# Attention blocks whose first score pairs are computed early: how many pairs go through VectorE, when, and where two output splits stand

## The chip, the cores and the metric

The kernel runs on one core of one Trainium2 chip. The metric is the device time of one execution in microseconds. Before the change it is 1400.34 us, the median of three runs (1400.21 to 1401.76). Everything said of single instructions comes from one profiled execution, which took 1400.11 us; its span, from the first to the last instruction of the program, is 1398.2 us.

## What is computed

The input x is 2048 tokens by 512 features in float32. It is layer-normalised; the result feeds a 32-head attention with head size 16 and a SwiGLU feed-forward of width 1792, and the output is a gated residual:

```python
x = A_x
xn = _layernorm(x, axis=-1)
s = _A_ref(xn, A_wqkv, A_wo)          # softmax attention, 32 heads, then @ wo
g = _silu(_B_ref(xn, B_w_gate, B_w_up, B_w_down))   # (silu(xn@gate) * (xn@up)) @ down
return x + s * g
```

## The kernel before, in words

After a prologue (normalisation and the q, k, v projections) the kernel goes through 32 attention **units** u. A unit is one group of four heads (8 groups) for one block of 512 queries (4 blocks). The 16 key tiles of a unit are cut into three **blocks** of 4 to 6 key tiles; that makes 96 blocks, numbered `now` = 0 to 95 (line 1038). In the last four units the blocks have 6, 6, 4 or 4, 6, 6 key tiles.

A block (`run`, line 963) handles 2n **score pairs**, two for each of its n key tiles; a pair is the scores of two heads for 128 keys and 512 queries. A pair takes one of two ways:

- **direct** (D): TensorE writes both heads' scores into one of two score slots, each two PSUM banks (`scored`, line 950), and ScalarE reads the slot and writes the exponentials to SBUF (line 954). The next pair but one needs the same slot again.
- **copied** (A, then B): TensorE writes one head's scores into a single spare bank, `acc[1]`; VectorE copies them to SBUF (line 1010); TensorE writes the other head's scores into the same bank, and VectorE copies those (line 1016). The exponential is taken in SBUF after all direct pairs of the block (line 1024).

In between TensorE does **fill** steps (F): a pair of matmuls on the upper and lower half of the array that belong to the feed-forward (line 187) or, in the last eight blocks, to the output projection (`project_out`, line 380). At the block's end come the value products of the block's key tiles (`values`, line 405, matmuls at line 409).

The order of D, A, B and F in a block is not written out by hand. `events` (line 511) gives each of them a mark on a scale of fill steps, sorts the marks, and puts fill steps in between. `f` is the number of fill steps of the block, `ahead` the number of pairs already computed. The fill steps per block are 11 and 10 in blocks 86 and 87, 18 in block 88, 24 in blocks 89, 90, 91, 94, 95 and 12 in 92 and 93.

Five blocks have score pairs put ahead (`begins`, line 493): 86, 87, 88, 92 and 93. Their first two direct pairs (`begin`, line 959) are computed between the value products of the block before: all its key tiles but the last, then the two pairs, then the last key tile (lines 1031 to 1034). Blocks 86, 87, 92 and 93 have four key tiles, block 88 has six.

VectorE's other work is kept in a list, `chores`, with a cost for each in fill steps. A chore is issued when the list of copies due (`copying`) leaves room for it (line 1020), or after the last copy of the block. Among the chores are:

- the finish of a unit (`normalise`, line 412): a transpose out of PSUM (line 420), a reciprocal (425), a product (429), and for every second group another transpose (445) with a split of the result (459, 456).
- the **output splits** (`split_out`, line 325): a [128, 512] part of the attention output is split into a rounded part (a cast) and a remainder (a subtraction, line 329) for block b of queries and quarter c. `out_splits` (line 354) says in which block each is issued, at the first A of that block.

`project_out(b)` multiplies these parts with the output weights. Block 88 holds 18 steps for the last block of queries, blocks 89 and 90 those of b = 0, blocks 91 to 93 those of b = 1, blocks 94 and 95 those of b = 2. Each product is made in two passes with the halves of the array swapped between the two banks; between the passes VectorE makes two copies of one element each (`turned_over`, line 384), and TensorE's second pass waits for them. After the second pass VectorE reads the banks (line 363) and GpSimd adds the residual (line 364). The parts are loaded from memory by `load_out` (line 308).

Of the kernel before, what the change touches and what calls it, by code (L numbers as in the profile page):

```python
# [51 lines left out]
def tile_block(ctx: ExitStack, tc: tile.TileContext, x, wqkv, wo, w_gate, w_up, w_down, out):  # L52
# [272 lines left out]
    def split_out(b, c):  # L325
        dst, src = lhs[b, c], parts_o[b, c]

        def rest():
            dve.tensor_sub(dst[1], src, dst[0].bitcast(F32))
            ready.add((b, c))  # L330

        chores.append((2, partial(dve.tensor_copy, dst[0], src)))
        chores.append((3, rest))
# [18 lines left out]
            load_gate()  # L352

    def out_splits():
        for b, c in {early: ((0, 0), (0, 1), (0, 2)), early + 2: ((1, 0), (1, 1)), early + 3: ((1, 2),),
                     early + 4: ((2, 0),), early + 5: ((2, 1),), early + 6: ((2, 2),)}.get(now, ()):
            split_out(b, c)
        if now == len(blocks) - 1:
            for j in range(EARLY):
                gate_rest(j)  # L360
# [39 lines left out]
    def gate_rest(t):  # L400
        chores.append((3, partial(dve.scalar_tensor_tensor, facc[:, t], facc[:, t], 0.5, gate[t], op0=ALU.mult, op1=ALU.mult)))
        chores.append((3, partial(dve.tensor_add, facc[:, t], facc[:, t], last[t])))
# [68 lines left out]
    now = -1  # L471
# [18 lines left out]
    early = len(sizes)  # L490
# [20 lines left out]
    def events(n, f, ahead):  # L511
        length = 2 * n - ahead + f
        need = 2 * n - max(2, (10 * length + 46) // 40)
        fit = 2 if ahead else (10 * length + 55) // 112
        copied = max(0, min(need, fit)) if now else 0
        direct = 2 * n - copied
        gap = max(4, min(5, (length - 8) / max(1, direct - 2)))
        marks = [] if ahead else [(0, "D"), (1, "D")]
        marks += [((0.5 if ahead else 7) + gap * i, "D") for i in range(direct - 2)]
        marks += [(2.2 + max(5.6, min(8, (length - 5) / (2 * copied))) * i, "AB"[i % 2]) for i in range(2 * copied)]  # L520
        marks.sort(key=lambda mark: mark[0] - 0.6 * (mark[1] == "D"))
        out = []
        at = left = 0
        for t, kind in marks:
            while left < f - (kind != "D") and at < t:
                out.append((at, "F"))
                left += 1
                at += 1
            out.append((at, kind))
            at += 1 if kind == "D" else 0.5  # L530
        return direct, out + [(at + i, "F") for i in range(f - left)]

    with ExitStack() as pro:
# [251 lines left out]
        copied = list(range(16))  # L785
# [155 lines left out]
    now = 0  # L941
# [21 lines left out]
    def run(u, first, n):  # L963
        nonlocal lower
        f = sizes.pop(0) if sizes else 0
        direct, todo = events(n, f, len(begun))
        if now == 0:
            for _ in range(4):
# [22 lines left out]
        for at, (t, e) in enumerate(todo):  # L991
            if at == final and not copying:
                tidy()
            if e == "F":
                fill(1)
            elif e == "D":
                probs[straight[done]] = scored(u, done % 2, *straight[done])
                done += 1
                if done == 2:
                    unit_end()  # L1000
            elif e == "A":
                if now > early and not turned_in:
                    turned_in.append(now)
                    out_splits()
                kt, j = copies.pop(0)
                waiting.append((kt, j))
                scores(u, spare_bank, kt, j, 0)
                lower = True
                probs[kt, j] = ppool.tile([P, 2, TB], F32, tag="pr", name="pr")
                dve.tensor_copy(probs[kt, j][:, 0], spare_bank)  # L1010
                free = copying.pop(0) + 3
            else:
                kt, j = waiting[-1]
                scores(u, spare_bank, kt, j, 1)
                lower = False
                dve.tensor_copy(probs[kt, j][:, 1], spare_bank)  # L1016
                free = copying.pop(0) + 3
# [8 lines left out]
        if not turned_in:  # L1026
            out_splits()
            tidy()
# [9 lines left out]
    for now, (u, first, n) in enumerate(blocks):  # L1038
        g, b = divmod(u, NB)
# [101 lines left out]
```

## Time and profile before

| | before |
|---|---|
| median of three runs | 1400.34 us |
| profiled execution | 1400.11 us |
| span of the profile | 1398.2 us |
| TensorE busy | 1388.8 us (99%) |
| ScalarE busy | 1087.9 us (78%) |
| VectorE busy | 760.9 us (54%) |
| GpSimd busy | 73.9 us (5%) |
| granted TensorE clock, mean | 1.000 |

Rows of a timeline give the start (us from the span's start), the duration, the engine (PE TensorE, ACT ScalarE, DVE VectorE, POOL GpSimd, SPq the queue of SyncE), the line of the kernel, the operation, what it writes and reads, and the count of merged instructions; in square brackets stands idle time of the engine ahead of it and what ended it. Matmuls overlap one another, so a step's cost is the distance of two starts and not the duration. Rows of the waits view give the waiting instruction, what released it, the sum, the count and the longest wait.

### The profile page before, as it was taken

The numbers are of one execution on the slowest core, as the hardware profiler recorded it, in microseconds if no ns is written. First come the engines' busy times: TensorE is split into PE (matmuls) and PEld (weight loads), VectorE is DVE, ScalarE is ACT, GpSimd is POOL, SyncE is SP. The second block draws the span as 40 slices with busy tenths as digits, with TensorE's granted clock in tenths as the row PEclk, the third lists the DMA queues.
The fourth block names the chain that finished last, engine by engine and source line by source line (L and its number), as shares of the span: only waits on it lengthen the run. The fifth ranks groups of instructions, "written<-read, shape, count | busy, mean of one in ns | idle before, by whom it ended". The sixth has DMA issues, their size and how long they took to land.

```text
span 1398.2 us, 27653 instructions
## 1 busy us (share of the span) xinstructions
PE 1388.8 (99%) x11193; PEld 848.9 (61%) x11193; DVE 760.9 (54%) x1299; ACT 1087.9 (78%) x1245; POOL 73.9 (5%) x92
## 2 busy tenths in 40 slices
PE   9999999999999999999999999999999999999998
PEld 7777755655665565566556556655565565564655
DVE  6674555455645653556445645554565446566454
ACT  6753678877888887787888778778877887788775
POOL 4200200000000000000000000000000000000222
PEclk9999999999999999999999999999999999999999
DMA  7778741043634511254514303356224112224323
GB/s 228 271 247 264 179 100 43 15 116 84 134 80 118 118 43 36 59 131 95 136 51 110 92 13 73 82 143 145 62 69 115 34 45 73 66 88 140 126 69 143
DMA packets 126953, 148.13 MB, mean 106 GB/s; under 512 B 12524, under 2 KB 79340, under 8 KB 126052
## 3 DMA queue, kind: packets, MB, share of 16 engines
q1 hardware_dynamic: 121620, 125.79, 34.9%
q0 software_dynamic: 4912, 20.12, 3.9%
q8 instruction: 89, 1.46, 0.4%
q14 instruction: 44, 0.36, 0.1%
q10 hardware_dynamic: 288, 0.39, 0.1%
HBM read 106.68 MB, written 39.58 MB: 105 GB/s over the span
## 4 chain that ended last, share of the span: by engine, by line
PE 87%; ACT 1%; DVE 1%; issue 0%; DVEq 0%; ACTq 0%
PE acc L409 32%; PE bankx L187 23%; PE score L948 16%; PE banky L187 9%; PE acc L948 3%; PE bankx L380 1%; ACT pr L954 1%; PE banky L380 1%; DVE pr L1010 0%; PE acc L1078 0%; PE bankx L1078 0%; DVE hh L1022 0%; PE score L1078 0%; DVE pr L1016 0%; DVE y L1085 0%
## 5 line engine op out<-in xcount | busy, mean ns | idle before, releaser
L954 ACT ACTIVATE pr<-score 128x1024 f32<-128x1024 f32 x857 | 810.2, 1032 | 226.2 <-PE score L948 224.3
L409 PE MATMUL acc<-pr,vst 128*17 128x512 f32 x4096 | 459.1, 593 | 0.0
L948 PE MATMUL score<-qst,kst 50*128 50x512 f32 x1714 | 393.5, 413 | 0.2 <-ACT pr L954 0.2
L187 PE MATMUL bankx<-fx,guh 64*128 64x512 f32 x896 | 333.3, 393 | 0.1
L187 PE MATMUL banky<-fx,guh 64*128 64x512 f32 x896 | 324.7, 393 | 0.0
L409 PEld LDWEIGHTS acc<-pr,vst 128*17 128x17 f32 x4096 | 110.0, 97 | 290.6 <-issue 271.0
L948 PEld LDWEIGHTS score<-qst,kst 50*128 50x128 f32 x1714 | 174.5, 184 | 143.9 <-issue 70.6
L1010 DVE COPY pr<-acc 128x512 f32<-128x512 f32 x167 | 115.5, 691 | 187.4 <-PE acc L948 183.6
L187 PE MATMUL bankx<-wd,hh 64*128 64x512 f32 x672 | 201.6, 392 | 0.0
L187 PE MATMUL banky<-wd,hh 64*128 64x512 f32 x672 | 198.3, 393 | 0.0
L187 PEld LDWEIGHTS bankx<-fx,guh 64*128 64x128 f32 x896 | 166.5, 186 | 18.7 <-issue 0.9
L187 PE MATMUL banky<-fx,gul 64*128 64x512 f32 x448 | 175.5, 392 | 0.0
L187 PE MATMUL bankx<-fx,gul 64*128 64x512 f32 x448 | 175.3, 391 | 0.0
L1024 ACT ACTIVATE pr<-pr 128x1024 f32<-128x1024 f32 x167 | 171.3, 1078 | 1.1 <-DVE turned_over L384 0.5
L187 PEld LDWEIGHTS banky<-fx,guh 64*128 64x128 f32 x896 | 166.4, 186 | 5.0
L1016 DVE COPY pr<-acc 128x512 f32<-128x512 f32 x167 | 115.4, 691 | 75.2 <-PE acc L948 61.4
L948 PE MATMUL acc<-qst,kst 50*128 50x512 f32 x334 | 134.4, 403 | 2.3 <-DVE pr L1010 2.2
L240 DVE SCALAR_TENSOR_TENSOR ga<-th,bankx 128x512 f32<-128x512 f32 x56 | 38.5, 687 | 178.5 <-ACT th L239 178.5
L187 PEld LDWEIGHTS bankx<-wd,hh 64*128 64x128 f32 x672 | 124.9, 186 | 13.9 <-DVE fx L1022 0.9
L187 PEld LDWEIGHTS banky<-wd,hh 64*128 64x128 f32 x672 | 124.3, 186 | 3.3
L187 PEld LDWEIGHTS bankx<-fx,gul 64*128 64x128 f32 x448 | 83.6, 187 | 10.1
L187 PEld LDWEIGHTS banky<-fx,gul 64*128 64x128 f32 x448 | 83.5, 186 | 2.7
(186 smaller groups left out, 1298.9 us busy)
## 6 DMA issues: line engine op xcount, KB each, us to landing
gur<-in_B_w_gate_dram SPq DMA_DIRECT2D x56, 256.0 KB
gur<-in_B_w_up_dram SPq DMA_DIRECT2D x56, 256.0 KB
wdr<-in_B_w_down_dram SPq DMA_DIRECT2D x56, 256.0 KB
kst<-k_d SPq DMA_DIRECT2D x192, 64.0 KB
qst<-q_d SPq DMA_DIRECT2D x192, 64.0 KB
fx<-xt_d SPq DMA_DIRECT2D x24, 512.0 KB
q_d<-parts SPq DMA_DIRECT2D x16, 512.0 KB
k_d<-parts SPq DMA_DIRECT2D x16, 512.0 KB
```

The source lines that it names most:

```text
L187: mm(banks[i], lhs[halves[i]], rhs[halves[i]], start=start, stop=stop)
L240: dve.scalar_tensor_tensor(ga, th, 1.0, bankx, op0=ALU.add, op1=ALU.mult)
L380: mm(banks[k], lhs[b, c][a][halves[h], (j + k) * P:(j + k + 1) * P], fx[halves[h], w, c], start=swap == i == 0, stop=i == 3 * n - 1, skip_ ...
L409: mm(acc[0][h * 32:h * 32 + DH + 1], v[:, kt % CT, h * (DH + 1):(h + 1) * (DH + 1)], probs[kt, h // 2][:, h % 2], start=kt == 0, stop=kt = ...
L948: mm(bank, k[r, j, kc * P:(kc + 1) * P], qst[u % 2][r, j], start=True, stop=True)
L954: act(pr, score[slot], AF.Exp, scale=0.25)
L1010: dve.tensor_copy(probs[kt, j][:, 0], spare_bank)
L1016: dve.tensor_copy(probs[kt, j][:, 1], spare_bank)
L1024: act(probs[kt, j], probs[kt, j], AF.Exp, scale=0.25)
```

## The change

Two places change. In `out_splits` the split (2, 0) moves from block 92 to block 91, (2, 1) from 93 to 92 and (2, 2) from 94 to 93. In `events`, for a block with pairs put ahead, the number of copied pairs becomes n - 3, and the first copied half gets the mark 0.3 instead of 2.2. Other blocks keep their marks.

```diff
     def out_splits():
-        for b, c in {early: ((0, 0), (0, 1), (0, 2)), early + 2: ((1, 0), (1, 1)), early + 3: ((1, 2),),
-                     early + 4: ((2, 0),), early + 5: ((2, 1),), early + 6: ((2, 2),)}.get(now, ()):
+        for b, c in {early: ((0, 0), (0, 1), (0, 2)), early + 2: ((1, 0), (1, 1)), early + 3: ((1, 2), (2, 0)),
+                     early + 4: ((2, 1),), early + 5: ((2, 2),)}.get(now, ()):
             split_out(b, c)
...
     def events(n, f, ahead):
         length = 2 * n - ahead + f
         need = 2 * n - max(2, (10 * length + 46) // 40)
-        fit = 2 if ahead else (10 * length + 55) // 112
-        copied = max(0, min(need, fit)) if now else 0
+        fit = (10 * length + 55) // 112
+        copied = n - 3 if ahead else max(0, min(need, fit)) if now else 0
         direct = 2 * n - copied
         gap = max(4, min(5, (length - 8) / max(1, direct - 2)))
         marks = [] if ahead else [(0, "D"), (1, "D")]
         marks += [((0.5 if ahead else 7) + gap * i, "D") for i in range(direct - 2)]
-        marks += [(2.2 + max(5.6, min(8, (length - 5) / (2 * copied))) * i, "AB"[i % 2]) for i in range(2 * copied)]
+        marks += [((0.3 if ahead else 2.2) + max(5.6, min(8, (length - 5) / (2 * copied))) * i, "AB"[i % 2]) for i in range(2 * copied)]
```

`early` is 88. Before the change the marks of the five blocks with pairs put ahead come out as follows (F fill, D direct pair, A and B the two halves of a copied pair):

```
86: F D F A F D F F F B D F F F D A F B F
87: F D F A F D F F F B D F F F D A B F
88: F D F A F D F F F D B F F F A D F F D F F B F D F F F D F D
92, 93: F D F A F D F F F B D F F F D A F F B F
```

## The prediction

> **What bounds the kernel now.** I read the page first (busy time, then the chain), then the waits of the stretch that the change touches, then the rows of TensorE (PE), ScalarE (ACT) and VectorE (DVE) in it.
>
> ```profile
> PE 1388.8 (99%) x11193; PEld 848.9 (61%) x11193; DVE 760.9 (54%) x1299; ACT 1087.9 (78%) x1245; POOL 73.9 (5%) x92
> ...
> PE 87%; ACT 1%; DVE 1%; issue 0%; DVEq 0%; ACTq 0%
> ```
>
> TensorE is busy 99% of the span and carries 87% of the chain that ended last. So an edit is worth what it takes out of TensorE's own queue as waiting, and nothing else. The diff reaches only the blocks whose first two score pairs are put ahead (86, 87, 88, 92, 93 of 96) and the output splits in blocks 91 to 94. All of that lies between 1261 and 1372 us. In that stretch the waits view says:
>
> ```profile
> PE acc L948 <- DVE pr L1010: 2.2, 4, 0.9
> ```
>
> TensorE waited four times for a VectorE copy out of the spare bank, once at the end of each of the four short blocks. TensorE's rows, with a block's first fill matmul, the late copied half, and the first value product:
>
> ```profile
> 1262.79 0.50 PE L187 MATMUL bankx<-wd,hh 64*128 64x512 f32 x1
> ...
> 1263.12 0.40 PE L948 MATMUL score<-qst,kst 50*128 50x512 f32 x2
> ...
> 1266.26 0.39 PE L948 MATMUL acc<-qst,kst 50*128 50x512 f32 x1
> ...
> 1267.44 0.50 PE L948 MATMUL acc<-qst,kst 50*128 50x512 f32 x1 [0.55 <-DVE pr L1010]
> ...
> 1268.10 2.77 PE L409 MATMUL acc<-pr,vst 128*17 128x512 f32 x24
> ...
> 1272.45 0.50 PE L187 MATMUL bankx<-wd,hh 64*128 64x512 f32 x1
> ...
> 1277.07 0.49 PE L948 MATMUL acc<-qst,kst 50*128 50x512 f32 x1 [0.85 <-DVE pr L1010]
> ...
> 1277.73 2.77 PE L409 MATMUL acc<-pr,vst 128*17 128x512 f32 x24
> ...
> 1282.08 0.50 PE L380 MATMUL bankx<-fx,part 64*128 64x512 f32 x1
> ...
> 1289.47 0.49 PE L948 MATMUL score<-qst,kst 50*128 50x512 f32 x2 [0.16 <-ACT pr L954]
> ```
>
> ```profile
> 1289.90 5.34 PE L409 MATMUL acc<-pr,vst 128*17 128x512 f32 x48
> ```
>
> ```profile
> 1338.56 0.50 PE L380 MATMUL bankx<-fx,wd 64*128 64x512 f32 x1
> ...
> 1340.08 0.39 PE L380 MATMUL bankx<-fx,wd 64*128 64x512 f32 x1
> ...
> 1340.54 0.39 PE L380 MATMUL bankx<-fx,wd 64*128 64x512 f32 x1
> ...
> 1343.25 0.49 PE L948 MATMUL acc<-qst,kst 50*128 50x512 f32 x1 [0.38 <-DVE pr L1010]
> ...
> 1343.91 2.77 PE L409 MATMUL acc<-pr,vst 128*17 128x512 f32 x24
> ...
> 1348.26 0.49 PE L380 MATMUL bankx<-fx,wd 64*128 64x512 f32 x1
> ...
> 1352.93 0.50 PE L948 MATMUL acc<-qst,kst 50*128 50x512 f32 x1 [0.39 <-DVE pr L1010]
> ...
> 1353.60 3.63 PE L409 MATMUL acc<-pr,vst 128*17 128x512 f32 x32
> ```
>
> From first fill to first value product a block now takes 5.31 us (86), 5.28 (87), 7.82 (88), 5.35 (92) and 5.34 (93). The next block's first fill follows 4.35 us later (1268.10 to 1272.45, 1277.73 to 1282.08, 1343.91 to 1348.26), since only value products and the two pairs ahead lie between; I keep that stretch as it is. A step (one fill pair, or one direct score pair) takes 0.23 us: 1340.08 to 1340.54 is two. The first step takes 0.33 (1262.79 to 1263.12). So step k of a block starts 0.33 + 0.23 x (k - 1) after its first fill. From the last direct pair to the value products it is 0.43 (1289.47 to 1289.90). A copied half takes half a step.
>
> **The change part by part.** Copied pairs become key tiles less three: 2 become 1 in the four blocks of four tiles, and 2 become 3 in block 88, which has six. Work on TensorE stays the same, as two halves are one step, like a direct pair. What moves is who waits for whom. VectorE and ScalarE:
>
> ```profile
> 1266.69 0.69 DVE L1010 COPY pr<-acc 128x512 f32<-128x512 f32 x1
> ```
>
> ```profile
> 1271.42 5.80 ACT L954 ACTIVATE pr<-score 128x1024 f32<-128x1024 f32 x6 [1.61 <-PE score L948]
> ```
>
> ```profile
> 1263.90 3.77 ACT L954 ACTIVATE pr<-score 128x1024 f32<-128x1024 f32 x4 [0.19 <-ACT pr L954]
> ```
>
> ```profile
> 1272.64 0.72 DVE L420 STREAM_TRANSPOSE o<-acc 128x512 f32<-128x512 f32 x1 [3.97 <-PE acc L409]
> ...
> 1273.39 0.25 DVE L425 RECIPROCAL rl<-o 128x16 f32<-128x16 f32 x1
> ```
>
> The spare bank's round is 1.18 us: half at 1266.26, copy at 1266.69, next half at 1267.44. Exps of direct pairs follow one another every 0.95 us (six in 5.80, one being 1.03), the first starting 1.03 us before the first fill (1271.42 against 1272.45). A direct pair uses a score slot that the exp two before it must have left.
>
> Block 86. The mark list of the new code, worked out by hand, is F D A F F D F B F F D F F F D F F D (F fill, D direct pair, A and B the copied halves). A stands at step 2 (0.56 us), B at step 6.5 (1.60), but the bank is free at 0.56 + 1.18 = 1.74: a wait of 0.14. The last D stands at step 16: 3.78 + 0.14 = 3.92. Its slot is free when the fifth exp ends: -1.03 + 4 x 0.95 + 1.03 = 3.80. No wait. Value products at 3.92 + 0.43 = 4.35 against 5.31: **0.96 gained**. If the third exp is late by 0.2 as at 1263.90, it is 0.75.
>
> Block 87, one F fewer. It opens with the finish of the last unit: transpose and reciprocal hold VectorE until 1273.64, 1.19 after the first fill, ahead of A's copy, which then ends at 1.92; B goes at 1.98 instead of 1.60, and TensorE, having drained, loses 0.10 more (0.33 for 0.23): 0.48. The third D is at step 9: 2.17 + 0.48 = 2.65; its exp starts after its 0.40 and about 0.1 for the hand-over (an estimate), at 3.15, and ends at 4.18. The last D (step 15, 3.55 + 0.48 = 4.03) waits for that slot until 4.20. Value products at 4.63 against 5.28: **0.65 gained**, between 0.3 and 1.0. What is late next is ScalarE, not the bank.
>
> Blocks 92 and 93 have one fill more between A and B. In 92, B is at step 7.5 (1.83), after 1.74: no wait; last D at step 17, 4.01; value products at 4.44 against 5.35: **0.91 gained**. 93 opens with a finish as 87 does: B at 1.98 for 1.83, so 0.15; 4.59 against 5.34: **0.75 gained**.
>
> Block 88 gets a third copied pair, list F D A F F D F B F F D F F A F D F F D B F F F D F A F D F B F. Three things happen. The first B waits 0.14 as in 86. The second A (step 12, 2.86 + 0.14 = 3.00) stands just ahead of the ninth fill, which ends the first pass of the output product; behind that fill TensorE needs the two tiny copies that turn the banks over (row 1328.17 below, 0.15 each), and these now queue on VectorE behind A's copy: 3.00 + 0.43 + 0.69 = 4.12, with the two about 4.35. TensorE would be at the tenth fill (step 14.5) at 3.58, so 0.8 of waiting and 0.1 for the restart. The third A (step 23) comes at 5.39 + 1.04 = 6.43, its B is due 3.5 steps (0.8) later but the bank is free only at 7.61, and from there to the value products it is 0.66 (1267.44 to 1268.10): 8.27 against 7.82: **0.45 lost**. Bounds: 0.9 lost if the two waits add to those that it has now, 0.5 gained if the turn-over gets ahead. Its twelve exps, the three out of SBUF last, end at -1.03 + 12 x 0.95 = 10.4 if fed without a gap; the last key tile's products begin at 8.27 + 5/6 of 5.34 = 12.7, so the third copied pair's exp costs nothing there unless it falls 2 us behind.
>
> The splits of the second block's and the third block's outputs (line 355): (2, 0) goes from block 92 to 91, (2, 1) from 93 to 92, (2, 2) from 94 to 93. Each is a cast and a subtraction on VectorE; no DMA is moved.
>
> ```profile
> 1357.73 0.39 PE L380 MATMUL bankx<-fx,hh 64*128 64x512 f32 x1
> ...
> 1366.56 5.34 PE L409 MATMUL acc<-pr,vst 128*17 128x512 f32 x48
> ```
>
> ```profile
> 1372.41 0.39 PE L380 MATMUL bankx<-fx,hh 64*128 64x512 f32 x1
> ```
>
> ```profile
> 1380.73 0.62 PE L409 MATMUL acc<-pr,vst 128*17 128x512 f32 x4
> ```
>
> ```profile
> 1290.56 0.42 DVE L143 CAST hh<-hh 128x512 fp32r<-128x512 f32 x1
> ```
>
> ```profile
> 1359.07 1.66 DVE L1022 CAST hh<-hh 128x512 fp32r<-128x512 f32 x1
> ```
>
> ```profile
> 1359.13 1.30 POOL L364 TENSOR_TENSOR pair<-facc,pair 128x512 f32<-128x512 f32 x1
> ```
>
> ```profile
> 1326.58 0.68 DVE L1016 COPY pr<-acc 128x512 f32<-128x512 f32 x1
> ...
> 1328.17 0.15 DVE L384 COPY turned_over<-bankx 1x1 f32<-1x1 f32 x1 [0.91 <-PE bankx L380]
> ```
>
> Block 94 needs 8.83 us to its value products, block 95, with the same marks and no such split, 8.32. In 94 the cast took 1.66 instead of 0.42, beside a GpSimd addition, and the fills that read its result queue behind it. With the split gone to 93, 94 should be like 95: **0.5 gained** (8.83 - 8.32); the lower bound is 0, if another wait stands behind it. In block 91 the added cast and subtraction start after the copy that ends at 1327.26 and end near 1328.4 (0.42 + 0.69), so the turn-over at 1328.17 comes up to 0.2 later, beside one copied half and one direct pair that cover part: **0.1 lost**, between 0 and 0.3. In 92 and 93 a split merely takes another's place.
>
> The Trainium skill, "SBUF — State Buffer", section "SBUF: two separate sides", says that VectorE and GpSimd share one port pair by an exclusive lock, held for a whole instruction. The stretched cast agrees: 1.66 us, ending 0.30 after GpSimd's addition ended at 1360.43. By that rule a moved split pays again wherever it meets such an addition; what this would cost is the second rival.
>
> The sum: 0.96 + 0.65 + 0.91 + 0.75 - 0.45 - 0.1 + 0.5 = **3.2 us**, 0.23%. The profiled execution took 1400.11 us (span 1398.2 and 1.9 around it), 0.23 below the median of 1400.34; I take the sum from the median: 1397.1.
>
> **The rivals.** First: ScalarE takes the bank's place. In a short block seven pairs instead of six now need a score slot. If exps follow at 1.22 (1.03 + 0.19, as before 1263.90) and not at 0.95, the fifth ends at 4.88, the value products start at 5.3, and the four blocks gain nothing; if half of them do so, about 1.6 us stay: 1398.7. For it speaks the 0.16 wait at 1289.47; against it the six exps in 5.80.
>
> Second: the slow cast moves along with the split. If a GpSimd addition met (2, 0) or (2, 2), that cast would again be 1.24 longer, and the 0.5 would be paid there: 3.2 - 0.5 = 2.7, 1397.6; were it to hold up a turn-over by the 0.8 worked out for block 88, 1.9, 1398.4. Against it: the additions wait for the output product's last bank reads, which in block 93 come behind the split in VectorE's queue.
>
> Third, slower: the split (2, 0) comes before its data.
>
> ```profile
> 1315.94 1.29 SPq L312 DMA_DIRECT2D hh<-o_d x3
> ```
>
> ```profile
> out_dram<-pair POOLq DMA_DIRECT2D x10, 256.0 KB, 2.9
> ```
>
> In block 91 it would read about 1327.3, 11.4 us after the load was issued (it now does so in block 92). A late landing would hold VectorE, and behind it the spare bank's copies and the turn-over, so TensorE, one for one. It takes back the gain at 14.6 us from issue and makes the kernel slower by over 0.2% at 17.4: 1403.1 or more. The nearest landing of that size is 2.9 us, so it is unlikely.
>
> Fourth: the change does not do what it says, because the waits at the block ends only pass to the next value products: 1400.
>
> **How the numbers follow.** Forecast as worked out: 0.70, of which 0.60 gains over 0.2% (2.8 us, about what a measurement of this kernel can tell from no change) and 0.10 less. First rival 0.16, second 0.06, third 0.04, fourth 0.04. That makes faster 0.60, same 0.10 + 0.16 + 0.06 + 0.04 = 0.36, slower 0.04. The terms at their ends (86: 0.6 to 1.0, 87: 0.3 to 1.0, 92: 0.7 to 0.95, 93: 0.5 to 0.95, 88: -0.9 to 0.5, 91: -0.3 to 0, 94: 0 to 0.5), not all at once, give a gain of about 1.4 to 4.3: 1396.0 to 1398.9, which takes in the likelier half of the first rival.
>
> **What would show it.** Right: the four waits of TensorE for the copy at line 1010 are gone; blocks 86, 87, 92, 93 take about 4.4, 4.6, 4.4, 4.6 us to their value products; 94 takes 8.3 with no cast over 0.5; 88 takes about 8.3 with a wait behind the turn-over. Wrong: the short blocks stay above 5 us with waits on ScalarE's exps, 88 loses over 1 us, or a cast of 1.6 shows in 91 to 93.

## The result, and the profile after

The changed kernel takes 1397.34 us (median of 14 runs, 1396.67 to 1398.52) against 1400.28 us for the kernel before, measured beside it (14 runs). The ratio is 0.9979, 95% interval 0.9971 to 0.9987: 2.9 us faster. The forecast was 1397.1, its range 1396.0 to 1398.9. The profiled execution took 1397.09 us, its span is 1395.3 us.

The page's first line and first engine of the changed kernel, and then what its waits view says of TensorE in the stretch 1262 to 1384 us (waiting instruction, releaser, sum, count, longest):

```profile
span 1395.3 us, 27643 instructions
...
PE 1387.7 (99%) x11193; PEld 849.8 (61%) x11193; DVE 755.9 (54%) x1293; ACT 1087.4 (78%) x1245; POOL 73.7 (5%) x92
```

```profile
PE bankx L380 <- DVE turned_over L384: 0.4, 1, 0.4
```

TensorE has as many instructions as before, VectorE six fewer: two copies less in each of four blocks, two more in block 88. The entry "PE acc L948 <- DVE pr L1010" with its four waits is gone, and a wait behind the turn-over is there instead. Now the ends of the short blocks in TensorE's timeline: first fill, last direct pair, first value product of blocks 86 and 87, and the first fill of 88.

```profile
1262.80 0.50 PE L187 MATMUL bankx<-wd,hh 64*128 64x512 f32 x1
...
1264.54 0.49 PE L948 MATMUL acc<-qst,kst 50*128 50x512 f32 x1
...
1264.88 0.40 PE L187 MATMUL banky<-wd,hh 64*128 64x512 f32 x1
...
1266.74 0.40 PE L187 MATMUL banky<-wd,hh 64*128 64x512 f32 x1
1266.92 0.50 PE L948 MATMUL score<-qst,kst 50*128 50x512 f32 x2
1267.35 0.62 PE L409 MATMUL acc<-pr,vst 128*17 128x512 f32 x4
...
1271.69 0.49 PE L187 MATMUL bankx<-wd,hh 64*128 64x512 f32 x1
...
1275.87 0.50 PE L948 MATMUL score<-qst,kst 50*128 50x512 f32 x2
1276.30 0.62 PE L409 MATMUL acc<-pr,vst 128*17 128x512 f32 x4
```

A direct pair now stands last, and 0.43 us behind it the value products begin. Block 88, at its turn-over and its end, on TensorE and then on VectorE:

```profile
1280.65 0.50 PE L380 MATMUL bankx<-fx,part 64*128 64x512 f32 x1
...
1283.68 0.49 PE L948 MATMUL acc<-qst,kst 50*128 50x512 f32 x1
...
1284.15 0.49 PE L948 MATMUL score<-qst,kst 50*128 50x512 f32 x2
1285.01 0.50 PE L380 MATMUL bankx<-fx,part 64*128 64x512 f32 x1 [0.37 <-DVE turned_over L384]
...
1287.05 0.45 PE L948 MATMUL acc<-qst,kst 50*128 50x512 f32 x1
...
1288.28 0.50 PE L948 MATMUL acc<-qst,kst 50*128 50x512 f32 x1
...
1288.93 0.62 PE L409 MATMUL acc<-pr,vst 128*17 128x512 f32 x4
```

```profile
1284.21 0.69 DVE L1010 COPY pr<-acc 128x512 f32<-128x512 f32 x1
1284.82 0.14 DVE L384 COPY turned_over<-bankx 1x1 f32<-1x1 f32 x1
1284.88 0.13 DVE L384 COPY turned_over<-banky 1x1 f32<-1x1 f32 x1
```

The copy of the second A (1283.68) runs until 1284.90, the two tiny copies end at 1285.01, and only then does the tenth fill start, although the direct pair before it started at 1284.15. The third A at 1287.05 and its B at 1288.28 are a bank round of 1.23 us apart. Last, block 94:

```profile
1355.30 0.39 PE L380 MATMUL bankx<-fx,hh 64*128 64x512 f32 x1
```

```profile
1363.63 0.62 PE L409 MATMUL acc<-pr,vst 128*17 128x512 f32 x4
```

From first fill to first value product, read in this way from each trace (us):

| block | 86 | 87 | 88 | 91 | 92 | 93 | 94 |
|---|---|---|---|---|---|---|---|
| before | 5.31 | 5.28 | 7.82 | 8.32 | 5.35 | 5.34 | 8.83 |
| forecast | 4.35 | 4.63 | 8.27 | 8.4 | 4.44 | 4.59 | 8.33 |
| after | 4.55 | 4.61 | 8.28 | 8.40 | 4.59 | 4.59 | 8.33 |
| splits alone | 5.32 | 5.28 | 7.80 | 8.40 | 5.33 | 5.34 | 8.34 |
| pairs alone | 4.56 | 4.61 | 8.27 | 8.32 | 4.57 | 4.59 | 8.31 |
| count alone | 4.48 | 4.31 | 8.29 | 8.40 | 4.43 | 4.47 | 8.35 |
| mark alone | 4.96 | 5.08 | 8.17 | 8.40 | 5.11 | 5.12 | 8.33 |
| short blocks only | 4.50 | 4.32 | 7.60 | 8.40 | 4.42 | 4.46 | 8.34 |
| 88 past the turn-over | 4.55 | 4.60 | 7.69 | 8.39 | 4.59 | 4.60 | 8.33 |
| copy ahead of the finish | 4.54 | 4.54 | 8.44 | 8.39 | 4.58 | 4.58 | 8.36 |
| exps of one head (86, 87) | 4.49 | 4.25 | 8.30 | 8.39 | 4.56 | 4.58 | 8.34 |
| best | 4.49 | 4.32 | 7.31 | 8.33 | 4.43 | 4.47 | 8.33 |

The stretch from these first value products to the next block's first fill is nearly the same in every trace: 4.33 to 4.36 us behind blocks 86, 87 and 92, as assumed, and 4.13 behind 93. The differences between the rows before and after add up to 0.76 + 0.67 - 0.46 - 0.08 + 0.76 + 0.75 + 0.50 = 2.90 us, which is the whole difference of the spans (1398.2 - 1395.3). So the table can stand for the time; it is the finer measure too, since in the traces here the first value products of all come between 162.8 and 164.0 us, and single times carry that difference.

### The profile page after: what moved, and what is told of

It is laid out like the page before. It is cut to its first block, busy times and chain, and to the rows that moved or that the text cites. A ratio compares the mean times of both kernels' runs of the same rounds, so it can differ in the third digit from the quotient of the medians.

```text
span 1395.3 us, 27643 instructions
## 1 busy us (share of the span) xinstructions
PE 1387.7 (99%) x11193; PEld 849.8 (61%) x11193; DVE 755.9 (54%) x1293; ACT 1087.4 (78%) x1245; POOL 73.7 (5%) x92
## 4 chain that ended last, share of the span: by engine, by line
PE 88%; ACT 0%; DVE 0%; issue 0%; DVEq 0%
PE acc L409 32%; PE bankx L187 23%; PE score L948 17%; PE banky L187 10%; PE acc L948 3%; PE bankx L380 2%; PE banky L380 1%; ACT pr L954 0%; PE acc L1078 0%; PE bankx L1078 0%; PE score L1078 0%; DVE pr L1010 0%; DVE y L1085 0%; DVE pr L1016 0%; DVE fx L1022 0%
## 5 line engine op out<-in xcount | busy, mean ns | idle before, releaser
L948 PE MATMUL score<-qst,kst 50*128 50x512 f32 x1720 | 395.4, 412 | 0.1
L948 PEld LDWEIGHTS score<-qst,kst 50*128 50x128 f32 x1720 | 176.3, 184 | 142.5 <-issue 66.3
L1010 DVE COPY pr<-acc 128x512 f32<-128x512 f32 x164 | 113.3, 691 | 188.1 <-PE acc L948 186.0
L1024 ACT ACTIVATE pr<-pr 128x1024 f32<-128x1024 f32 x164 | 168.0, 1078 | 0.0
L1016 DVE COPY pr<-acc 128x512 f32<-128x512 f32 x164 | 113.3, 691 | 74.9 <-PE acc L948 65.9
L948 PE MATMUL acc<-qst,kst 50*128 50x512 f32 x328 | 131.9, 402 | 0.1
```

Source lines behind the costliest of these rows:

```text
L948: mm(bank, k[r, j, kc * P:(kc + 1) * P], qst[u % 2][r, j], start=True, stop=True)
L1024: act(probs[kt, j], probs[kt, j], AF.Exp, scale=0.25)
```

## The experiments

**The two edits apart.** The first kernel is that before with only line 355 of the change, the second the changed one with line 355 as before.

```diff
-early + 3: ((1, 2),), early + 4: ((2, 0),), early + 5: ((2, 1),), early + 6: ((2, 2),)
+early + 3: ((1, 2), (2, 0)), early + 4: ((2, 1),), early + 5: ((2, 2),)
```

> The kernel before with only the output splits moved. Theory (each term stands by itself: block 94 loses 0.5 us because its split's cast is stretched beside a GpSimd addition, and no other block can suffer the same): block 94 takes 8.3 us from its first fill to its value products instead of 8.83, block 91 at most 0.1 more, all other blocks as before; time about 0.4 us below the kernel before, 1399.9. Rival (the stall passes to the block that takes the split): 94 takes 8.3, but 92 or 93 takes 0.3 to 0.5 more than 5.35 and 5.34, and the time is that of before.

> The changed kernel with the output splits where they were before. Theory: blocks 86, 87, 92, 93 take 4.55, 4.61, 4.58, 4.59 us to their value products and 88 takes 8.28, as in the changed kernel, and 94 is at 8.8 again; time about 2.5 us below the kernel before, 1397.8. Rival (the two edits need each other, since the shorter blocks 92 and 93 leave VectorE less room for the splits): one of 92, 93, 94 takes over 0.3 more than that, gain under 2.2.

Splits alone: 1399.78 us, ratio 0.9998 (0.9989 to 1.0007); that interval does not tell 0.4 us from nothing, but the table does: 94 at 8.34, 91 0.08 longer, the others as before. Pairs alone: 1397.37 us, ratio 0.9980 (0.9970 to 0.9989), as fast as the whole change. And here both the theory and its rival fall: block 94 takes 8.31 us although it still holds its split. GpSimd's and VectorE's rows of the kernel with the pairs alone:

```profile
1353.52 1.27 POOL L364 TENSOR_TENSOR pair<-facc,pair 128x512 f32<-128x512 f32 x1 [16.61 <-DVE facc L363]
...
1355.67 1.29 POOL L364 TENSOR_TENSOR pair<-facc,pair 128x512 f32<-128x512 f32 x1
```

```profile
1356.38 0.69 DVE L1010 COPY pr<-acc 128x512 f32<-128x512 f32 x1 [2.35 <-PE acc L948]
1356.98 0.42 DVE L1022 CAST hh<-hh 128x512 fp32r<-128x512 f32 x1
```

The cast takes 0.42 us. With two copies fewer in block 93, VectorE reads the output banks earlier (line 363 from 1352.75, 2.9 us ahead of block 94's first fill, against 1.5 before the change), GpSimd's second addition starts 0.03 us after block 94's first fill (1355.64) instead of 1.4 after it (1359.13 against 1357.73), and it ends at 1356.96, 0.03 ahead of the cast at 1356.98. So the two edits take away the same 0.5 us, and each would do it without the other.

**Is it GpSimd's addition that stretches the cast?** The kernel before, with two residual additions left out:

```diff
-        pool.tensor_add(xr[t], gt[t % NT], xr[t])
-        (pool if t < end - 1 else sp).dma_start(out[rows[t]], xr[t])
+        if t in (6, 7):
+            pool.dma_start(out[rows[t]], gt[t % NT])
+        else:
+            pool.tensor_add(xr[t], gt[t % NT], xr[t])
+            (pool if t < end - 1 else sp).dma_start(out[rows[t]], xr[t])
```

> The kernel before, with the last two residual additions of the second block of queries left out (its two tiles are stored without x), so that GpSimd adds nothing while block 94 begins; splits and pairs as before. Theory (the cast in block 94 is stretched only because a GpSimd addition runs beside it): the cast takes 0.42 us, and block 94 takes 8.3 instead of 8.83; time 0.5 below the kernel before. Rival (the cast waits for its data or for memory traffic, or the split in this block costs TensorE by itself): the cast stays above 1 us, or 94 stays above 8.6.

In the kernel before, TensorE's ninth and tenth fill of block 94, the tenth being the first that reads this split:

```profile
1360.33 0.39 PE L380 MATMUL bankx<-fx,hh 64*128 64x512 f32 x1
...
1360.78 0.50 PE L380 MATMUL bankx<-fx,hh 64*128 64x512 f32 x1
```

The cast ended at 1360.73, and the tenth fill starts 0.45 us behind the ninth instead of 0.23. About 0.3 more goes at the next copied half: it starts at 1362.11, 0.52 behind the fill ahead of it, since VectorE's copy that frees its bank (1361.37 to 1362.05) was queued behind the cast and its subtraction.

VectorE's row of that split in the kernel without the two additions (the edit shifts lines behind it by three):

```profile
1359.58 0.42 DVE L1025 CAST hh<-hh 128x512 fp32r<-128x512 f32 x1
```

The cast takes 0.42 instead of 1.66 us, block 94 takes 8.35 us (1358.24 to 1366.59), and no other block's time to its value products differs by over 0.1 us from the kernel before. The theory holds. The one time was 1400.31 beside 1400.41; the first value products came 0.08 us later than in the profiled execution before, the blocks from there to 85 took 0.4 us longer, and the end behind block 95 another 0.3, so that time says nothing of the 0.5.

**Count and mark apart.** The changed kernel with the first mark back at 2.2; and with two copied pairs but the early mark.

```diff
-        marks += [((0.3 if ahead else 2.2) + max(5.6, ...
+        marks += [(2.2 + max(5.6, ...
```

> The changed kernel with the first copied half's mark back at 2.2 in all blocks. Theory (the gain of the short blocks comes from the count alone: a direct pair stands last, so no copy is waited for at the end; the early mark only makes the second half wait in the middle): with A at step 3 and B at step 8.5 the bank is free in time, 86 takes 4.5, 87 takes 4.35 (limited by the fifth exp), 92 and 93 take 4.5; block 88 now ends D A B F, so its last half waits 1.0 us, and takes 8.3 to 8.6. Rival (the early mark is what gains): the short blocks stay at 5.0 or more.

```diff
-        copied = n - 3 if ahead else max(0, min(need, fit)) if now else 0
+        copied = 2 if ahead else max(0, min(need, fit)) if now else 0
```

> The changed kernel with two copied pairs in every block with pairs put ahead, as before the change, and the early mark. Theory (what counts is how many steps stand between a copied half and the next one, against a bank round of 1.18 us): 86 ends A D F F B F, 3.5 steps, a wait of 0.4 to 0.5, so 4.8 to 4.9; 87 ends A D F B F, 2.5 steps, 4.9; 92 and 93 end A D F F F B F, 4.5 steps, 4.6 to 4.7; 88 has its second half ahead of the ninth fill again and takes 8.0 or more. Rival (the count is what gains): the short blocks stay at 5.2 or more.

Count alone, 1396.40 us in one run, has shorter short blocks than the change: 4.31 instead of 4.61 in block 87. There A stands one step later, and B two steps later, so B no longer waits for the bank. Block 88 is as long as after the change, for another reason, seen in TensorE's rows of its end:

```profile
1286.71 0.39 PE L948 MATMUL acc<-qst,kst 50*128 50x512 f32 x1
...
1287.88 0.49 PE L948 MATMUL acc<-qst,kst 50*128 50x512 f32 x1 [0.78 <-DVE pr L1010]
1288.54 0.62 PE L409 MATMUL acc<-pr,vst 128*17 128x512 f32 x4
```

Its last two halves stand side by side and cost a full bank round (1.17 us). The early mark loses in the short blocks and spares 88 this. Mark alone (1399.07 us in one run) gains 0.35 us in 86, where the count alone gains 0.83, and 0.2 in the other short blocks; blocks 92 and 93 at 5.11 were forecast at 4.6 to 4.7. The rows of block 92 in that kernel, TensorE then VectorE, show what the forecast left out:

```profile
1340.24 0.50 PE L948 MATMUL acc<-qst,kst 50*128 50x512 f32 x1
...
1341.52 0.50 PE L948 MATMUL acc<-qst,kst 50*128 50x512 f32 x1
...
1342.87 0.50 PE L948 MATMUL acc<-qst,kst 50*128 50x512 f32 x1
```

```profile
1340.77 0.69 DVE L1016 COPY pr<-acc 128x512 f32<-128x512 f32 x1 [0.26 <-PE acc L948]
1341.38 0.68 DVE L329 TENSOR_TENSOR hh<-hh 128x512 fp32r<-128x512 f32 x1
1342.12 0.69 DVE L1010 COPY pr<-acc 128x512 f32<-128x512 f32 x1
```

I had counted the steps between the last two halves alone, 4.5. But the half before them waits as well, and the split's subtraction gets ahead of its copy, so the rounds are 1.28 and 1.35 us, one behind the other.

**Block 88 apart.** The changed kernel with one copied pair in the short blocks and two in block 88, mark 2.2; and the changed kernel with block 88's first mark at 1.3.

```diff
-        copied = n - 3 if ahead else max(0, min(need, fit)) if now else 0
+        copied = (1 if n == 4 else 2) if ahead else max(0, min(need, fit)) if now else 0
...
-        marks += [((0.3 if ahead else 2.2) + max(5.6, ...
+        marks += [(2.2 + max(5.6, ...
```

> The changed kernel with one copied pair in the blocks of four key tiles, and block 88 with two copied pairs as before, the mark back at 2.2. Theory (the third copied pair in block 88 is a loss of 0.45 us, and the early mark costs the short blocks some 0.3 in all): 86 4.5, 87 4.35, 88 7.8, 92 and 93 4.5; 0.8 us below the changed kernel, 1396.5, 3.8 below the kernel before. Rival (block 88 needs the third copied pair once the blocks ahead are shorter, since ScalarE comes to it with less rest): 88 takes 8.2 or more, and the time is that of the changed kernel.

```diff
-        marks += [((0.3 if ahead else 2.2) + max(5.6, ...
+        marks += [(((0.3 if n == 4 else 1.3) if ahead else 2.2) + max(5.6, ...
```

> The changed kernel with the first mark of block 88 at 1.3 instead of 0.3: it keeps three copied pairs, but its second copied half now stands behind the ninth fill and no longer ahead of it, so that the two tiny copies of the turn-over are ahead of that half's copy on VectorE. Theory: the wait of 0.8 behind the turn-over falls to 0.1, the last half still waits some 0.6: 88 takes 7.6 to 7.7 instead of 8.28. Rival (block 88 is long because three copied pairs are too many for VectorE or ScalarE): 88 stays at 8.1 or more.

Short blocks only: 1396.38 us, ratio 0.9973 (0.9962 to 0.9983), and 88 at 7.60: its third copied pair is a loss, of 0.68 us against the changed kernel. 7.8 had been expected, as before the change; where the other 0.2 comes from no run separates, but ScalarE's first exps for block 88 stand 1.04 us ahead of its first fill here, and 0.77 before the change. 88 past the turn-over: 7.69 us with three copied pairs, 1396.76 us in one run. So it is not the third pair as such that costs. VectorE's and TensorE's rows:

```profile
1284.19 0.14 DVE L384 COPY turned_over<-bankx 1x1 f32<-1x1 f32 x1 [0.38 <-PE bankx L380]
1284.29 0.15 DVE L384 COPY turned_over<-banky 1x1 f32<-1x1 f32 x1
1284.43 0.69 DVE L1010 COPY pr<-acc 128x512 f32<-128x512 f32 x1
```

```profile
1286.69 0.40 PE L948 MATMUL acc<-qst,kst 50*128 50x512 f32 x1
...
1287.88 0.49 PE L948 MATMUL acc<-qst,kst 50*128 50x512 f32 x1 [0.32 <-DVE pr L1010]
```

The tiny copies now precede the big one, and of the added waits only that at the end is left.

**What is late next in block 87.** First the finish's chores out of the way of A's copy, then shorter exps.

```diff
-        free = 0
+        free = copying[0] if begun_here else 0
```

> The changed kernel, where VectorE's chores in blocks with pairs put ahead are issued only behind the first copied half's copy, so that the unit's finish (transpose, reciprocal) no longer stands ahead of it. Theory: in block 87 the second half goes at 1.74 us after the first fill instead of 1.80 to 1.98, in 93 it no longer waits: 87 takes 4.35 to 4.4 instead of 4.61, 93 takes 4.45; block 88 may lose up to 0.3 because the feed-forward's last additions come later. Rival (ScalarE's exps set the end of block 87): 87 stays within 0.1 of 4.61.

```diff
-        act(pr, score[slot], AF.Exp, scale=0.25)
+        act(pr[:, :heads], score[slot][:, :heads], AF.Exp, scale=0.25)   # heads = 1 in blocks 86 and 87
...
-                   probs[kt, h // 2][:, h % 2], ...
+                   probs[kt, h // 2][:, 0 if now in (86, 87) else h % 2], ...
```

> The changed kernel, where blocks 86 and 87 take the exponentials of only one head of each direct pair and use them for the other head too, so that an exp takes about 0.6 us instead of 1.03; the matmuls are the same in number and size. Theory (the last direct pair of 86 and 87 waits for the exp that must leave its slot): the waits go, 86 takes 4.4 instead of 4.55 and 87 takes 4.35 to 4.45 instead of 4.61. Rival (what is left over is TensorE's own restart behind the copied half): both stay within 0.05 of what they are.

The finish mattered little: 87 at 4.54 instead of 4.61, the rival's side, and 93 at 4.58, where the theory had 4.45. 88 came out 0.16 longer, within what was expected; the feed-forward's last addition comes later there (1278.70 against 1277.23). Short exps: 87 at 4.25, so ScalarE held its end; that is 0.1 more than was expected. ScalarE's rows of block 87 in the changed kernel, and in the one with exps of one head:

```profile
1274.78 1.96 ACT L954 ACTIVATE pr<-score 128x1024 f32<-128x1024 f32 x2 [0.31 <-PE score L948]
```

```profile
1274.44 0.60 ACT L954 ACTIVATE pr<-score 128x512 f32<-128x512 f32 x1 [0.32 <-PE score L948]
```

In the changed kernel the fifth exp ends at 1275.81 (two overlapped in 1.96 us, from 1274.78), and the last direct pair goes at 1275.87. In block 86 short exps gained 0.06 only, where 0.15 was expected. The end of that block with exps of one head:

```profile
1267.81 0.60 PE L948 MATMUL score<-qst,kst 50*128 50x512 f32 x2
...
1268.34 2.77 PE L409 MATMUL acc<-pr,vst 128*17 128x512 f32 x24
```

The last pair starts 3.96 us after the first fill (1263.85), against 4.12 in the changed kernel, but its two halves are 0.2 apart (0.60 for the row instead of 0.50), and the value products follow it by 0.53 instead of 0.43.

**The best.** What these runs point to: one copied pair in the short blocks at mark 2.2, two in block 88 at mark 1.3, splits left where they were.

```diff
-        copied = n - 3 if ahead else max(0, min(need, fit)) if now else 0
+        copied = (1 if n == 4 else 2) if ahead else max(0, min(need, fit)) if now else 0
...
-        marks += [((0.3 if ahead else 2.2) + max(5.6, ...
+        marks += [((1.3 if ahead and n == 6 else 2.2) + max(5.6, ...
```

> What the runs so far point to: one copied pair in the blocks of four key tiles with the first mark at 2.2, two copied pairs in block 88 with the first mark at 1.3 (its second copied half then stands behind the turn-over, and 5.5 steps behind the half before it, so it waits neither for the bank nor holds the turn-over), and the output splits where they were before. Theory: 86 4.5, 87 4.3, 88 7.2 to 7.3, 91 8.32, 92 and 93 4.4 to 4.5, 94 8.33 to their value products; 4.6 us below the kernel before, 1395.7, and 1.6 below the changed kernel. Rival (block 88 is held by ScalarE's exps and not by the bank): 88 stays at 7.6, 1396.1.

1395.96 us, where 1395.7 was expected, ratio to the kernel before 0.9968 (0.9956 to 0.9980), and 88 at 7.31 as expected. The rows of block 88's copied halves:

```profile
1281.22 0.39 PE L948 MATMUL acc<-qst,kst 50*128 50x512 f32 x1
...
1282.40 0.50 PE L948 MATMUL acc<-qst,kst 50*128 50x512 f32 x1
...
1283.81 0.39 PE L948 MATMUL acc<-qst,kst 50*128 50x512 f32 x1
...
1285.49 0.39 PE L948 MATMUL acc<-qst,kst 50*128 50x512 f32 x1
...
1287.96 1.48 PE L409 MATMUL acc<-pr,vst 128*17 128x512 f32 x12
```

They stand 1.18, 1.41 and 1.68 us apart: the first B comes a bank round behind its A, the others later, and the waits view shows no wait of TensorE in this stretch. Against the changed kernel the blocks of the table are 1.7 us shorter (0.06 + 0.29 + 0.97 + 0.07 + 0.16 + 0.12 + 0). The two were not timed beside each other, and the intervals of their ratios overlap, so that this is the faster of the two rests on the table.

The best kernel also shows the cast of block 94 beside GpSimd's addition once more. GpSimd, VectorE, and TensorE's tenth fill:

```profile
1354.47 1.31 POOL L364 TENSOR_TENSOR pair<-facc,pair 128x512 f32<-128x512 f32 x1
```

```profile
1355.32 0.77 DVE L1022 CAST hh<-hh 128x512 fp32r<-128x512 f32 x1
```

```profile
1356.81 0.39 PE L380 MATMUL bankx<-fx,hh 64*128 64x512 f32 x1
```

The cast takes 0.77 us and ends 0.30 behind the addition, as in the kernel before, but 0.72 ahead of the fill that reads it, and block 94 takes 8.33.

## Why the prediction was right, and where it was not

**The waits at the block ends** were the gain. The four short blocks gained 2.94 us (0.76, 0.67, 0.76, 0.75) where 3.27 was worked out, and the wait on the copy at line 1010 left the list.

**Block 86** came out at 4.55 and not 4.35. The prediction gave 0.14 of waiting for B and nothing for the restart; the fill behind B came 0.34 after it, so this short wait was followed by the 0.1 that I had allowed only in block 87. Then the last pair waited for the late fifth exp until 1266.92. The run with short exps puts that wait at 0.06; without it the last pair still starts 0.04 later than worked out (3.96 for 3.92), and its halves are out of step, which costs 0.1. So that the prediction's alternative (0.75 gained, by a late exp) comes out as 0.76 is luck.

**Block 87** hit 4.61 against 4.63, but by a partly wrong route. B went at 1.80 us and not at 1.98, since A's copy started at 1272.81, under the reciprocal's tail, and not behind it:

```profile
1272.64 0.25 DVE L425 RECIPROCAL rl<-o 128x16 f32<-128x16 f32 x1
1272.81 0.63 DVE L1010 COPY pr<-acc 128x512 f32<-128x512 f32 x1
```

The next direct pair's halves then started 0.24 apart (1274.06 and 1274.30), so its exp, the fifth, still came at 3.09 where 3.15 was worked out. The figure was right because the fifth exp set the end, which the shortened exps show; moving the finish away gained 0.07.

**Blocks 92 and 93**: in 92 the steps took a little over 0.23 (the last pair at 4.07, not 4.01), and that pair's two halves ran out of step (0.58 instead of 0.50), which delayed the value products by 0.1. In 93 the figure is right, 4.59, but by luck: B came at 1.82, where it was due, so the 0.15 of waiting behind the finish was not there, and with the finish moved behind A's copy (4.58) the block is no shorter. The last pair stood at 4.06 and its halves out of step (0.60), as in 92, and that made up for it.

**Block 88** lost 0.46 where 0.45 was worked out, by the two waits that were named: the tenth fill comes 1.33 us after the second A (1283.68 to 1285.01), where 2.5 steps would be 0.58, so 0.75 is lost with the restart, and the last B comes a whole bank round after its A.

**The splits** are the step that failed. The prediction said that with the split gone to 93, block 94 should be like 95, and added 0.5 for it beside the pairs. The 0.5 is there, and its cause, a cast beside GpSimd's addition, is shown by the kernel without the additions. But with the pairs changed, that addition is over before the cast starts, and the split in block 94 costs nothing; the edit of line 355 then gives only what it costs in block 91 (0.08 forecast as 0.1). I had bounded that term from below by 0 "if another wait stands behind it", and had not carried the shorter block 93 forward to GpSimd's start. As both edits were made, the sum came out the same.

**The rivals.** ScalarE took the bank's place in blocks 86 and 87 in part, for 0.06 and 0.36 us; the last pair starts 4.12 and 4.18 us after the first fill there, and 3.96 and 3.71 with short exps. The four blocks keep nine tenths of the gain. The slow cast did not move along. Nothing shows the split (2, 0) waiting for its load: its cast starts at 1326.19, before the copy ahead of it has ended (1326.27), and block 91 is 0.08 longer.

In the Trainium skill, "SBUF — State Buffer", section "SBUF: two separate sides", the shared port pair is an exclusive lock for a whole instruction. The runs agree: the cast took 1.66 us beside an addition that ended at 1360.43, 0.77 beside one that ended at 1355.79, the cast ending 0.30 behind the addition both times, and 0.42 when the addition ended 0.03 us earlier or was left out. In the kernel before, the cast is recorded from 1359.07 and the addition from 1359.13, but VectorE's copy ahead of the cast ended only at 1359.15.

## What to carry to other kernels

When two engines pass one buffer to and fro, count the steps of the busy engine between two uses against the full round (here 1.18 us), and count each round from where the last one really ended. A tiny operation that releases another engine (here a one-element copy) must be queued ahead of a long one, not behind it. Two edits that remove the same wait do not add: carry the earlier edit's shift forward to every engine before pricing the next.

## What was not expected of the hardware

TensorE pays about 0.1 us (0.34 between two starts instead of 0.23) even after a wait of 0.1 to 0.2 us, as behind B at 1264.54. And a cast that meets GpSimd's addition need not cost anything: in the best kernel it met one and took 0.77 us, and block 94 was as short as with the addition over, since the cast still ended 0.72 us ahead of the fill that reads it. In the kernel before, it ended 0.05 us ahead of that fill, which had waited for it.
